# Two edits beside a fused attention and MLP kernel: staging loads issued earlier, and the positive half of an ELU taken by VectorE

## The chip, the cores and the metric

The kernel runs on one core of a Trainium2 chip. Its time is the device time of one execution in microseconds; the time given for a kernel is the median of several executions. Engines are named as in the profile: PE (TensorE), DVE (VectorE), ACT (ScalarE), POOL (GpSimd) and SP (SyncE, which here issues DMAs).

## The reference

Three stages follow each other. An attention with pooled queries (4 batches, 8 heads, 1152 keys, 576 pooled queries, head size 64) gives 2304 tokens of 512 values. A dense MLP multiplies them by a 512x2048 matrix, applies an ELU and multiplies by a 2048x512 matrix. A mixture of 8 experts (512 to 1024 to 512) with top-1 routing follows.

```python
scores = scale * (q_pool @ k.T); attn = softmax(scores); x = attn @ v
h = x @ w_in
g = where(h > 0, h, exp(min(h, 0)) - 1)
y = g @ w_out
# route every row of y to the expert with the largest logit, then
out = gate * (relu(y @ w1[e]) @ w2[e])
```

w_in and w_out arrive as 64-bit floating point words, so the kernel turns them into 32-bit numbers by integer operations on the chip.

## The kernel before

Every product of 32-bit numbers is done in three matmuls over a high and a low part of each operand (H and L). The high part is a rounded copy, usually by ACT, and the low part is the difference, by DVE or POOL.

**Attention** (lines 30 to 330) takes the 16 pairs of heads one after another; a pair is 9 steps, one for each 128 pooled queries, so there are 144 steps, numbered g, and t is the step within its pair (g = 9i + t). The order of the work within a step is written out by hand in SEQ (line 17), and every engine and every DMA queue works in that order. Scores of step g+2 are made (qk, line 164), their maximum is taken by DVE (smax), ACT takes the exponential, PE transposes the probabilities (tp), ACT and DVE split them (evH, evL), and matmuls with v come later from a queue (av_ops). The transposed keys of the next pair, the tile kst, are put together by four DMAs per head from SP: head 0 in step t=4 (D0) and head 1 in step t=7 (D1), both at the operation named inv near the end of a step. PE first reads the new head 0 in step t=7.

Beside the attention, at the operation named dec (line 320), which is third in a step or nearly so, two lists are worked off. The first, pre, decodes weights: two loads of 512 KB into two halves of a staging tile dx (lines 346 and 348), then for each block five DVE operations (lines 351 to 361), an ACT copy and a POOL subtraction or a store; from g=10 on some operations are taken in the steps named in DEC. The second, xops, comes when the first is empty (g=100): for each of the first two chunks of tokens, X.load(n) (line 380) brings attention results from memory into dx, 4 DMAs of 384 KB for chunk 0 and 8 DMAs for chunk 1, and split_ops makes 4 POOL sums (line 417) and 4 splits (lines 419 and 420). The 18 entries are spread evenly up to g=140: X.load(0) falls to g=103 (t=4), its first sum to g=105, X.load(1) to g=123 (t=6).

**The dense MLP** (moe1, line 427) works on 7 chunks of 256 or 384 tokens and on 16 blocks f of 128 hidden values. A unit is a chunk and a block. The first 32 units alternate chunk 0 (384 columns) and chunk 1 (256 columns), because the weight blocks are still being decoded. In unit n PE makes L1 (12 matmuls into a PSUM bank h, of which there are two), then elu runs on it, and PE makes L2 of unit n-3. The elu is min(h,0) by ACT (em), a tanh and an exponential by ACT, one DVE operation that joins them (line 455), and the sum with max(h,0). In chunks 2 to 6 that sum is a second DVE operation that reads h (line 460). In chunks 0 and 1 ACT makes max(h,0) with another pass over h (line 450) into a ring tile, and POOL adds (line 457). The split of the result (gH by ACT, gL by POOL, lines 463 and 464) is queued in fin and issued two units later.

Each elu of the first 32 units also takes two entries of the list dec: words, the five DVE operations of one block of weights and the load of the block after next, and parts, the ACT copy and the POOL subtraction (lines 363 and 365) of the block before. Eight blocks (AHEAD) were decoded beside the attention, so their units have no DVE words; 20 blocks have them.

Of the kernel before, what the change touches and what calls it, by code (L numbers as in the profile page):

```python
# [10 lines left out]
F32=mybir.dt.float32; F32R=mybir.dt.float32r; I32=mybir.dt.int32; U32=mybir.dt.uint32; I64=mybir.dt.int64; BF16=mybir.dt.bfloat16  # L11
AF=mybir.ActivationFunctionType; ALU=mybir.AluOpType; AX=mybir.AxisListType
# [17 lines left out]
def attention(tc, q, k, v, xS, rS, ident, pairs=None, extra=(), start=lambda: None):  # L30
    nc=tc.nc
# [4 lines left out]
    with ctx:  # L36
# [18 lines left out]
        def load(i,what="qkv",eng=None):  # L55
            if i>=len(pairs): return
            b,hp=pairs[i]; h0=2*hp
            d=D_.setdefault(i,dict(ks={},vs={},kst={}))
            for w in what:
                if w=='q':  # L60
                    t=d['qn']=ld.tile([128,KT,2,D],F32,name="qn")
                    (eng or nc.sync).dma_start(out=t,in_=q[b,h0:h0+2].rearrange("h (s r) d -> (h s) (r d)",r=2).rearrange("(t p) x -> p t x",p=128))
                else:
                    t=d[w+'n']=ld.tile([128,2,KT,D],F32,name=w+"n")
                    (eng or nc.sync).dma_start(out=t,in_={'k':k,'v':v}[w][b,h0:h0+2].rearrange("h (p t) d -> p h t d",p=128))
# [98 lines left out]
        def qk(g,n):  # L164
            i,t=divmod(g,9); d=D_[i]
            if g not in st: new(g)
            A=QA[i%2]; Bq=QB[i%2]
            if t==4: L=[(512,0),(640,1)]
            else: L=[(128*t,0)] if t<4 else [(128*t+128,1)]
            ops=[(w[:,c:c+128],h) for c,h in L for w in (A,Bq)]  # L170
            if n==0:
                o=psS.tile([128,2,512],F32,name="Sa"); st[g]['S'][0]=o[:,:,0:384]
                outs=[(o[:,j,0:384],j) for j in range(2)]
            else:
                o=psU.tile([128,384],F32,name="Sb"); st[g]['S'][1]=o
                outs=[(o,2)]
            for o,j in outs:
                for x,(w,h) in enumerate(ops):
                    nc.tensor.matmul(o,w,d['kst'][h][:,j*384:(j+1)*384],start=(x==0),stop=(x==len(ops)-1))  # L179
        def smax(g,n):  # L180
            s=st[g]
            nc.vector.tensor_reduce(out=s['nm'][:,n:n+1],in_=s['S'][n],axis=AX.XY if n==0 else AX.X,op=ALU.max,negate=True)  # L182
        def bias(g):
            nm=st[g]['nm']
            nc.vector.tensor_reduce(out=st[g]['bs'],in_=nm,axis=AX.X,op=ALU.min)  # L185
# [11 lines left out]
        def invT(i,h):  # L197
            a,b=TS[h]; bb,hp=pairs[i]; n=b-a
            T=psT.tile([128,384],F32,name="T",tag="T")
            nc.tensor.transpose(T[0:n,0:128],inv.pop((i,h))[:,1,0:n],ident)  # L200
            o=sm.tile([5,128],F32,name="ro",bufs=1)
            nc.scalar.copy(out=o[0:n],in_=T[0:n,0:128])
            flat=rS[bb][hp:hp+1].rearrange("o h s -> (o h s)")
            nc.sync.dma_start(out=flat[128*a:128*b].rearrange("(t p) -> t p",p=128),in_=o[0:n])
        def invB(i,h):
            bb,hp=pairs[i]
            flat=rS[bb][hp:hp+1].rearrange("o h s -> (o h s)")
            r=rB[i,h]=sm.tile([128,576],F32,name="rB",bufs=2)
            nc.sync.dma_start(out=r,in_=flat[576*h:576*h+576].partition_broadcast(128))
# [48 lines left out]
        N=len(pairs); NG=9*N  # L258
        load(0,'q'); load(0,'k'); load(0,'v',nc.gpsimd)
        def take(l,n=1):  # L260
            for _ in range(n):
                if l: l.pop(0)()
        ops={}
        def do(i,*names):

            if i>=N: return
            if i not in ops: ops[i]=pool_ops(i,i==0)|prep_ops(i)
            for n in names:
                o=ops[i].pop(n,None)
                if o: o()  # L270
# [10 lines left out]
        def takeav(n):  # L281
            while avq and n>0:
                avq[0].pop(0)(); n-=1
                if not avq[0]: avq.pop(0)
        stores=[]; g0=None
        for g in range(NG+4):
            i,t=divmod(g,9)
            if g<NG:
                if t==2 and i>0: load(i+1,'v')
                if t==2: load(i+2,'q')  # L290
                if t==5: load(i+2,'k')
            f2=g+2<NG; f0=g<NG
            if not f0:
                while avq: takeav(99)
            for op in SEQ[t in EARLY]:
                a=op[:-1]; n=op[-1]
                if op=='scl':
                    if g in at: x,y=at.pop(g); x(); stores.append((g,y))
                elif op=='st':
                    while stores and (stores[0][0]<g or not f0): stores.pop(0)[1]()  # L300
                elif op=='inv':
                    if f0 and t in (3,7): invT(i,t//4)
                    if t==5 and f0: invB(i,0)
                    if t==0 and i>0: invB(i-1,1)
                    for di,x in SPQ.get(t,()): f0 and do(i+di,x)
                    if g==0: do(1,'q0')
                elif not f0: pass
                elif a=='q': f2 and qk(g+2,int(n))
                elif a=='m': f2 and smax(g+2,int(n))
                elif a=='e': f2 and exp(g+2,int(n))  # L310
                elif op=='bias': f2 and bias(g+2)
                elif a=='t': tp(g,int(n))
                elif a=='c': evH(g,int(n))
                elif op in ('av','aw'): takeav((AVN[t]+(op=='av'))//2)
                elif a=='l': evL(g,int(n))
                elif op=='sum':
                    if t in (3,7): ssum(i,t//4)
                elif op in ('pool','prep'):
                    for di,n in (POOL if op=='pool' else PREP).get(t,()): do(i+di,n)
                elif op=='dec':  # L320
                    n=DEC.get(t,0) if g>9 else 0
                    while n and extra[0]:
                        d,x=extra[0].pop(0); x(); n-=d
                    if not extra[0]:
                        if g0 is None: g0=g
                        want=min(NX[1],NX[1]*(g-g0)//(140-g0)); take(extra[1],want-(NX[1]-len(extra[1])))
                else: raise Exception(op)
            if f0:
                for c in DONE.get(t,[]): avq.append(av_ops(i,c))
# [97 lines left out]
def moe1(tc, X, yS, R, Wt, dec, rpool, psX, temps, plan, ops, setup, spare):  # L427


    nc=tc.nc  # L430
    ep,gp,psH,psY=temps
    rp=rpool
# [10 lines left out]
    def elu(c,f):  # L443
        h=hs.pop((c,f)); N=CHUNKS[c][1]; h=h[:,:N]
        m=ep.tile([128,384],F32,name="em",bufs=2); t=ep.tile([128,384],F32,name="et",bufs=3); m_,t_=m[:,:N],t[:,:N]
        nc.scalar.activation(out=m_,in_=h,func=AF.Relu,scale=-1.0)  # L446
        if c<2:

            r_=rp.tile([128,512],F32,name="yt",bufs=4)[:,:N]
            nc.scalar.activation(out=r_,in_=h,func=AF.Relu)  # L450
        nc.scalar.activation(out=t_,in_=m_,func=AF.Tanh,scale=-0.5)
        nc.scalar.activation(out=m_,in_=m_,func=AF.Exp,scale=-1.0)  # L452
        if len(fin)>1: fin.pop(0)()
        if c<2: take(dec,1)
        nc.vector.scalar_tensor_tensor(out=t_,in0=m_,scalar=1.0,in1=t_,op0=ALU.add,op1=ALU.mult)  # L455
        if c<2:
            nc.gpsimd.tensor_tensor(out=t_,in0=r_,in1=t_,op=ALU.add)
            take(dec,1)
        else:
            nc.vector.scalar_tensor_tensor(out=t_,in0=h,scalar=0.0,in1=t_,op0=ALU.max,op1=ALU.add)  # L460
        def parts():
            gH=gp.tile([128,384],F32R,name="gH",bufs=2); gL=gp.tile([128,384],F32R,name="gL",bufs=2); gs[c,f]=(gH,gL)
            nc.scalar.copy(out=gH[:,:N],in_=t_)  # L463
            nc.gpsimd.tensor_tensor(out=gL[:,:N],in0=t_,in1=gH[:,:N].bitcast(F32),op=ALU.subtract)  # L464
        fin.append(parts)
# [10 lines left out]
    yt={}  # L476
# [63 lines left out]
    for n in range(len(units)+LAG):  # L540
        if n<len(units):
            c,f=units[n]; nxt=c+1
# [11 lines left out]
        if n>=LAG:  # L554
            c,f=units[n-LAG]
# [23 lines left out]
def take(l,n):  # L579
    for _ in range(n):  # L580
        if l: l.pop(0)()
# [300 lines left out]
def full(tc,q,k,v,w_in,w_out,emb,tau,w1,w2,out,dbg=None):  # L882
    nc=tc.nc
# [6 lines left out]
    with contextlib.ExitStack() as ctx:  # L890
        c=pool(ctx,"c")
# [6 lines left out]
        with tc.manual_schedule():  # L898
# [10 lines left out]
            X=XChunks(nc,xS,[df[:,1536*n:1536*n+1536].rearrange("p (k n) -> p k n",k=4) for n in range(2)])  # L909
# [11 lines left out]
                pre+=[(j<5,x) for j,x in enumerate(ops[n][1])]  # L921
                if n+2<len(ops): pre.append((0,ops[n+2][0]))
            xops=[]
            for n in range(2): xops+=[lambda n=n: X.load(n)]+X.split_ops(n)
            attention(tc,q,k,v,xS,rS,ident,extra=(pre,xops),start=norms)
            wp2=pool(right,"w2",side="right")
            W0.append(wp2.tile([128,2,1024],F32R,name="W2",tag="W2"))
# [1 line left out]
            rp=pool(ctx,"m_r",2)  # L929
# [14 lines left out]
            dec=[]  # L944
# [37 lines left out]
            with contextlib.ExitStack() as tmp:  # L982
# [4 lines left out]
                n=lambda i: i<NSTATIC  # L987
# [56 lines left out]
```

## Time and profile before

| What | us |
|---|---|
| median of three executions | 1339.13 (1337.27 to 1340.05) |
| the profiled execution | 1333.49 |
| its span, first to last instruction | 1331.7 |
| attention | about 0 to 573 |
| dense MLP, chunks 0 and 1 | about 577 to 729 |
| dense MLP, chunks 2 to 6 | about 729 to 1040 |
| experts | about 1040 to 1331 |

Busy time over the span: PE 1225.0, DVE 1080.6, ACT 899.8, POOL 625.0 us. A row of the timeline begins with the start and the duration of an instruction in us; a bracket at its end is the engine's idle time before it and what ended that. In the rows of the windows each engine has its busy time and, in brackets, its instructions; then come the granted TensorE clock as a share of full speed, the mean busy share of the DMA engines and GB/s.

### The profile page before, as it was taken

Reading aid. Unit: us, or ns where it says so; the run is one execution under the profiler, and the core shown is the slowest. Engines: PE = TensorE matmul, PEld = TensorE weight load, DVE = VectorE, ACT = ScalarE, POOL = GpSimd, SP = SyncE. Lnnn points to the kernel's source line nnn. Section 1 sums busy time; section 2 is a strip of 40 time slices with the busy share of each in tenths; the row PEclk is TensorE's granted clock in tenths of the full one; section 3 lists DMA queues with packets and bytes.
Section 4 is the critical chain, followed back from the end, with each engine's and each line's share of the span. In section 5 each row is a group of like instructions: output and inputs, shape, how many; then the busy total and the mean of one; then the engine's idle time right before and its main releaser. Section 6 shows DMA issues by size and latency. Waiting matters only on the chain. (4 is left out here: it accounts for less than half of the span.)

```text
span 1331.7 us, 22409 instructions
## 1 busy us (share of the span) xinstructions
PE 1225.0 (92%) x7341; PEld 1084.4 (81%) x7341; DVE 1080.6 (81%) x1970; ACT 899.8 (68%) x2059; POOL 625.0 (47%) x567
## 2 busy tenths in 40 slices
PE   5889999999999999978779989999999999999996
PEld 4778888888988899866668978888888887788885
DVE  5689999999998788868896797657576889998993
ACT  6778888888888788855546645454556667676672
POOL 3435455444444555347676433333342444455552
PEclk9989999999999899999989999999999999999998
DMA  5446666666666557233432201100102223258710
GB/s 175 115 120 175 159 159 168 168 177 184 167 155 157 152 147 162 70 107 109 118 105 71 86 24 41 28 32 25 39 11 109 82 97 110 95 216 326 264 36 22
DMA packets 121928, 158.53 MB, mean 119 GB/s; under 512 B 12391, under 2 KB 94199, under 8 KB 117456
## 3 DMA queue, kind: packets, MB, share of 16 engines
q1 hardware_dynamic: 117536, 145.13, 38.6%
q0 software_dynamic: 3696, 11.34, 2.4%
q8 instruction: 60, 0.98, 0.3%
q10 hardware_dynamic: 576, 0.59, 0.1%
q14 instruction: 60, 0.49, 0.1%
HBM read 157.58 MB, written 22.37 MB: 135 GB/s over the span
## 5 line engine op out<-in xcount | busy, mean ns | idle before, releaser
L235 DVE TENSOR_TENSOR PL<-T,PH 128x384 fp32r<-128x384 f32 (+1 forms) x480 | 220.7, 509 | 28.5 <-ACT PH L233 28.3
L441 PE MATMUL h<-xH,W 128*128 128x384 f32 (+1 forms) x896 | 222.8, 319 | 15.1 <-DVE et L460 12.5
L233 ACT CAST PH<-T 128x384 fp32r<-128x384 f32 (+1 forms) x480 | 187.3, 457 | 69.6 <-PE T L222 67.7
L464 POOL TENSOR_TENSOR gL<-et,gH 128x384 fp32r<-128x384 f32 (+1 forms) x112 | 111.9, 999 | 202.2 <-ACT gH L463 110.0
L829 DVE TENSOR_TENSOR W<-sg,W 128x2048 fp32r<-128x2048 f32 (+1 forms) x84 | 192.4, 2324 | 16.3 <-ACT W L828 10.7
L441 PEld LDWEIGHTS h<-xH,W 128*128 128x128 f32 x896 | 159.1, 192 | 27.1 <-DVE et L460 20.5
L222 PE MATMUL T<-ident,P 128*128 128x128 f32 x1296 | 168.3, 275 | 0.0
L245 PE MATMUL O<-PH,vs 128*128 128x256 f32 (+1 forms) x576 | 166.4, 311 | 0.6 <-ACT xo L248 0.6
L446 ACT ACTIVATE em<-h 128x384 f32<-128x384 f32 (+1 forms) x112 | 49.9, 446 | 162.0 <-PE h L441 154.3
L245 PE MATMUL O<-PL,vs 128*128 128x256 f32 (+1 forms) x576 | 159.1, 299 | 0.0
L222 PEld LDWEIGHTS T<-ident,P 128*128 128x128 f32 x1296 | 151.6, 141 | 7.4 <-ACT KX L135 1.2
L182 DVE TENSOR_REDUCE nm<-Sa 128x1 f32<-128x768 f32 x144 | 136.5, 948 | 16.2 <-PE Sa L179 12.3
L189 ACT ACTIVATE P<-Sa,bs 128x768 f32<-128x768 f32 x144 | 131.4, 913 | 24.5 <-DVE bs L185 20.2
L441 PE MATMUL h<-xL,W 128*128 128x384 f32 (+1 forms) x448 | 141.8, 316 | 0.0
L455 DVE SCALAR_TENSOR_TENSOR et<-em,et 128x384 f32<-128x384 f32 (+1 forms) x112 | 66.5, 598 | 88.6 <-ACT em L452 86.7
L179 PE MATMUL Sa<-kst,qa 128*128 128x384 f32 x320 | 114.5, 358 | 23.3 <-ACT P L189 23.3
L828 ACT CAST W<-sg 128x2048 fp32r<-128x2048 f32 (+1 forms) x63 | 114.2, 1836 | 11.0 <-DMA sg<-moe_w 11.0
L472 PE MATMUL y<-W,gH 128*128 128x512 f32 x288 | 114.6, 398 | 3.1 <-ACT gH L463 3.1
L475 PE MATMUL y<-W,gL 128*128 128x512 f32 x288 | 87.1, 402 | 28.5 <-POOL gL L464 28.5
L473 PE MATMUL y<-W,gH 128*128 128x512 f32 x288 | 112.9, 392 | 0.0
L250 POOL TENSOR_TENSOR xo<-xo,rB 128x256 f32<-128x256 f32 (+1 forms) x64 | 52.1, 814 | 124.4 <-DMA rB<-rS 87.7
L245 PEld LDWEIGHTS O<-PH,vs 128*128 128x128 f32 x576 | 109.3, 190 | 1.1 <-ACT xo L248 1.1
(298 smaller groups left out, 2975.2 us busy)
## 6 DMA issues: line engine op xcount, KB each, us to landing
sg<-moe_w SPq DMA_DIRECT2D x80, 1024.0 KB
qn<-q SPq DMA_DIRECT2D x16, 576.0 KB
kn<-k SPq DMA_DIRECT2D x16, 576.0 KB
rB<-rS SPq DMA_DIRECT2D x32, 288.0 KB
vn<-v SPq DMA_DIRECT2D x15, 576.0 KB
dx<-moe_w_in SPq DMA_DIRECT2D x16, 512.0 KB
dx<-moe_w_out SPq DMA_DIRECT2D x16, 512.0 KB
qb<-qa SPq DMA_DIRECT2D x64, 96.0 KB
```

What stands on the lines that cost most here:

```text
L179: nc.tensor.matmul(o,w,d['kst'][h][:,j*384:(j+1)*384],start=(x==0),stop=(x==len(ops)-1))
L182: nc.vector.tensor_reduce(out=s['nm'][:,n:n+1],in_=s['S'][n],axis=AX.XY if n==0 else AX.X,op=ALU.max,negate=True)
L189: nc.scalar.activation(out=o,in_=s['S'][n],func=AF.Exp,bias=s['bs'],scale=1.0,accum_out=s['su'][:,n:n+1])
L222: nc.tensor.transpose(T[:,n*128:(n+1)*128],P[:,kt*128:(kt+1)*128],ident)
L233: for H,L,src in parts(g,j): nc.scalar.copy(out=H,in_=src)
L235: for H,L,src in reversed(list(parts(g,j))): nc.vector.tensor_tensor(out=L,in0=src,in1=H.bitcast(F32),op=ALU.subtract)
L245: nc.tensor.matmul(O[0][:,:n],vs[:,kt].rearrange("p a d -> p (a d)"),R[:,kt,:n],start=first,stop=last)
L441: nc.tensor.matmul(h[:,:N],a,b[:,k,:N],start=(n==0),stop=(n==11)); n+=1
L472: nc.tensor.matmul(y,gH[:,sl],wH,start=(f==0),stop=False)
L473: nc.tensor.matmul(y,gH[:,sl],wL,start=False,stop=False)
L828: else: nc.scalar.copy(out=H[:,q],in_=s[:,q])
L829: (nc.gpsimd if (w,j,h) in self.pool_L else nc.vector).tensor_tensor(out=L[:,q],in0=s[:,q],in1=H[:,q].bitcast(F32),op=ALU.subtract)
```

## The change

In attention the first two entries of pre, the loads of the first two weight blocks, are taken in step g=4 instead of g=10. X.load(n) is followed by three empty entries, and xops is taken one entry per step from g=112 on: X.load(0) is then in g=112 (t=4), its first sum in g=116; X.load(1) in g=124 (t=7), its first sum in g=128; the last entry is in g=135. In the MLP the ACT pass and the POOL addition of chunks 0 and 1 go, and DVE's operation of line 460 is used in all chunks.

```diff
                 elif op=='dec':
                     n=DEC.get(t,0) if g>9 else 0
+                    if g==4:
+                        for _ in range(2): extra[0].pop(0)[1]()
                     while n and extra[0]:
                         d,x=extra[0].pop(0); x(); n-=d
                     if not extra[0]:
                         if g0 is None: g0=g
-                        want=min(NX[1],NX[1]*(g-g0)//(140-g0)); take(extra[1],want-(NX[1]-len(extra[1])))
+                        if g>=max(g0,112) and extra[1]: take(extra[1])
...
         nc.scalar.activation(out=m_,in_=h,func=AF.Relu,scale=-1.0)
-        if c<2:
-
-            r_=rp.tile([128,512],F32,name="yt",bufs=4)[:,:N]
-            nc.scalar.activation(out=r_,in_=h,func=AF.Relu)
         nc.scalar.activation(out=t_,in_=m_,func=AF.Tanh,scale=-0.5)
         nc.scalar.activation(out=m_,in_=m_,func=AF.Exp,scale=-1.0)
         if len(fin)>1: fin.pop(0)()
         if c<2: take(dec,1)
         nc.vector.scalar_tensor_tensor(out=t_,in0=m_,scalar=1.0,in1=t_,op0=ALU.add,op1=ALU.mult)
-        if c<2:
-            nc.gpsimd.tensor_tensor(out=t_,in0=r_,in1=t_,op=ALU.add)
-            take(dec,1)
-        else:
-            nc.vector.scalar_tensor_tensor(out=t_,in0=h,scalar=0.0,in1=t_,op0=ALU.max,op1=ALU.add)
+        nc.vector.scalar_tensor_tensor(out=t_,in0=h,scalar=0.0,in1=t_,op0=ALU.max,op1=ALU.add)
+        if c<2: take(dec,1)
...
-            for n in range(2): xops+=[lambda n=n: X.load(n)]+X.split_ops(n)
+            for n in range(2): xops+=[lambda n=n: X.load(n)]+[lambda: None]*3+X.split_ops(n)
```

## Rows read from the trace of the kernel before

**Rows 1.** The page: the span.

```profile
span 1331.7 us, 22409 instructions
```

**Rows 2.** Waits, 60 to 80 us: who waited for whom, total, times, longest.

```profile
DVE dx L351 <- DMA dx<-moe_w_in: 8.5, 1, 8.5
...
PE Sa L179 <- ACT P L189: 8.4, 1, 8.4
```

**Rows 3.** Timeline of SP's DMA issues: start, duration, line, what.

```profile
39.48 0.66 SPq L112 DMA_DIRECT2D kst<-KH  x1
...
54.45 0.43 SPq L204 DMA_DIRECT2D rS<-ro  x1
...
62.75 0.43 SPq L346 DMA_DIRECT2D dx<-moe_w_in  x1
...
81.80 0.28 SPq L204 DMA_DIRECT2D rS<-ro  x1
...
420.97 0.28 SPq L204 DMA_DIRECT2D rS<-ro  x1
...
421.77 3.11 SPq L380 DMA_DIRECT2D dx<-xS  x4
...
443.20 0.43 SPq L204 DMA_DIRECT2D rS<-ro  x1
...
461.11 0.28 SPq L204 DMA_DIRECT2D rS<-ro  x1
...
476.44 0.43 SPq L204 DMA_DIRECT2D rS<-ro  x1
```

**Rows 4.** Windows of 1 us in the attention: engines, clock, DMA share, GB/s.

```profile
69.00:70.00 1.00, 0.00 (x0) 0.00 (x0) 0.96 (x3) 0.00 (x0) 0.00 (x0) 0.50 1.06 385
428.00:429.00 1.00, 1.00 (x11) 1.00 (x10) 0.86 (x2) 0.55 (x3) 0.00 (x0) 1.00 1.11 223
436.00:437.00 1.00, 1.00 (x5) 1.00 (x4) 0.81 (x3) 0.00 (x0) 0.00 (x0) 0.50 1.14 297
```

**Rows 5.** Timeline of PE: first scores of a pair, early and after X.load(0).

```profile
48.55 0.34 PE L179 MATMUL Sb<-kst,qa 128*128 128x384 f32 x1
...
435.03 0.69 PE L179 MATMUL Sb<-kst,qa 128*128 128x384 f32 x1 [4.47 <-DMA kst<-KX]
```

**Rows 6.** Window over the 28 units of the MLP in which words run.

```profile
578.90:712.50 133.60, 103.33 (x530) 87.71 (x529) 113.94 (x133) 71.79 (x167) 94.17 (x86) 0.96 0.36 104
```

**Rows 7.** Waits, 577 to 730 us.

```profile
PE y L475 <- POOL gL L464: 28.5, 17, 2.7
...
DVE dx L351 <- DMA dx<-moe_w_in: 8.1, 4, 4.7
...
DVE dx L351 <- DMA dx<-moe_w_out: 5.6, 4, 2.0
```

**Rows 8.** Timeline of DVE and POOL, one unit's words beside POOL's work.

```profile
609.70 1.49 POOL L365 TENSOR_TENSOR W<-yt,W 128x512 fp32r<-128x512 f32 x1
...
610.06 1.68 DVE L355 SCALAR_TENSOR_TENSOR dx<-dx 128x512 int32<-128x512 int32 x1
...
611.13 1.48 POOL L464 TENSOR_TENSOR gL<-et,gH 128x384 fp32r<-128x384 f32 x1
...
611.77 1.39 DVE L357 SCALAR_TENSOR_TENSOR dx<-dx 128x512 int32<-128x512 int32 x1
...
613.27 0.69 DVE L361 SCALAR_TENSOR_TENSOR yt<-dx 128x512 f32<-128x512 int32 x1
```

**Rows 9.** Lines 457 and 460: duration ns min/median/max, first and last start, forms.

```profile
L457 POOL TENSOR_TENSOR et<-yt,et x32: 733/1042/1340, 585.1 to 728.8; 128x384 f32<-128x384 f32 x16, 128x256 f32<-128x256 f32 x16
...
L460 DVE SCALAR_TENSOR_TENSOR et<-h,et x80: 424/557/559, 731.1 to 1044.9; 128x384 f32<-128x384 f32 x48, 128x256 f32<-128x256 f32 x32
```

**Rows 10.** Timeline of DVE: two units without words between, and chunk 2.

```profile
594.38 0.89 DVE L455 SCALAR_TENSOR_TENSOR et<-em,et 128x384 f32<-128x384 f32 x2
...
738.07 0.56 DVE L455 SCALAR_TENSOR_TENSOR et<-em,et 128x384 f32<-128x384 f32 x1 [2.39 <-ACT em L452]
```

## The prediction

> **What bounds the kernel now.** I read the page first: the span is 1331.7 us [rows 1] and the profiled execution took 1333.49, so 1.8 us lie around it. Its shares of busy time say that PE leads, but they are averages, so I went on by stage: the waits of each stretch, then the timelines where a wait stands out.
>
> Attention is paced by PE, except at two places. At 60 us DVE, whose queue also holds the maxima that the softmax needs, waits 8.5 us for a weight load that SP issued only at 62.75; everything stops with it, and PE stands idle for 8.4 us [rows 2, 3]. The price is best read from marks that recur in each pair, SP's store of the sums (line 204, in steps t=3 and t=7): from t=7 to the next t=3 it took 81.80-54.45 = 27.35 us here, against 461.11-443.20 = 17.91 elsewhere [rows 3], a loss of 9.4 us. That is more than the idle time because PE's granted clock was at 0.50, its lower level of 1.2 GHz, when it began again [rows 4]. The second place is at 430: PE waits 4.47 us for the new keys (kst) [rows 5], whose DMAs were issued behind the four of X.load(0). From t=3 to t=7 it took 443.20-420.97 = 22.23 us, against 476.44-461.11 = 15.33 one pair later [rows 3]: a loss of 6.9 us, again with the clock at 0.50 behind it [rows 4].
>
> In the first two chunks of the MLP PE is busy for only 103 of 133.6 us [rows 6], and waits for POOL's gL, 28.5 us in 17 times [rows 7]. POOL is not the root: DVE is busy for 113.9 and POOL for 94.2 of the same 133.6 us [rows 6], and they hinder each other. A DVE word operation with two inputs from SBUF takes 0.69 us where POOL is idle. The one at 611.77 took 1.39: POOL's subtraction ended at 611.13+1.48 = 612.61, 0.84 us after the start, and the DVE operation ended 0.55 us later; the one at 610.06, begun under another POOL operation, took 1.68 [rows 8]. So each waits until the other has finished. DVE paces the stage, and much of its busy time is waiting for POOL.
>
> **The change, part by part.**
>
> 1. *The first two loads in g=4.* The operation that waited finds its data there long before; the wait, its idle PE and the slow clock after it go: -9.4 us. What is late next there is nothing the rows show; the steps after it ran at the usual pace. But the loads are now queued on SP directly ahead of the first pair's key DMAs: these are issued from 39.48 on, and PE first reads the keys at 48.55 [rows 3, 5], 9.1 us later. X.load(0), some 1.57 MB by its shapes, needed 435.03-421.77 = 13.3 us from its first issue to the keys behind it [rows 3, 5]; at the 223 GB/s of that stretch [rows 4] it took 7.0 of them, which leaves 6.2 for the keys. The two loads are 1.05 MB: 2.7 us at the 385 GB/s at which the same loads moved at 69 us, 4.7 at 223 [rows 4]. The keys then come 8.9 to 10.9 us after the first issue: in time, or 1.8 us late. I take +0.5, and keep 6.9 us (the loss of the other place) as the bad end.
>
> 2. *X.load(0) from g=103 to g=112, X.load(1) from g=123 to g=124.* Both g=103 and g=112 are steps t=4, and in both dec stands ahead of inv, so the four DMAs of X.load(0) are again directly ahead of the key DMAs, which are again needed in t=7. The three empty entries part the load from POOL's first sum, not from the keys. I therefore expect the second stall to move one pair on, to about 470 us, and cost the same: 0 net, with -6.9 as the other end. X.load(1), 8 DMAs, now stands ahead of head 1's keys; those are read only four steps later (some 15 us at 33 to 34 us for 9 steps), against the 13.3 us of the larger load above: 0. It also waits for POOL's last split, one step before; SP's later issues in the list need later work anyway. POOL's stall on the first sum goes, but nothing in the waits of that stretch waited for it: 0.
>
> 3. *ACT's pass and POOL's sum go, DVE reads h* (units 0 to 27, the window of rows 6; the last four units have no words there, and DVE has slack: 0).
>  - Added: 28 operations of line 460, 557 ns for 384 columns and 424 for 256 [rows 9]. Back to back two such operations hide 0.08 us (0.89 for 0.554+0.413, the two forms of line 455 [rows 10]): 14 x (0.48+0.34) = +11.5 us. Their largest time in 80 is 559 ns although POOL works beside many of them [rows 9]: one input comes from PSUM, and they don't wait for POOL.
>  - Relieved: 28 POOL sums of 0.733 us (256 columns, the smallest) or about 1.04 (the median, for 384) [rows 9] = 24.9 us of POOL. DVE was busy 0.853 of the window [rows 6], and of a word operation 0.55 of 0.69 us needs what POOL holds [rows 8]: 24.9 x 0.853 x 0.80 = -17.0 us of waiting inside DVE's operations.
>  - DVE's waits for loads, 8.1+5.6 us in 8 times [rows 7], stand behind units without words. There two more operations now lie between a load's issue and its use, 0.82 us, and of the shortest waits (0.38, 0.73) all goes: -5.7.
>  - A new wait: h is released by DVE and not by ACT, with two banks. L1 of unit n+2 begins after DVE's second operation of unit n; behind it on PE stands L2 of unit n-1. Where words run DVE then has two units of about 4.8 us before it needs the result, and L1 (2.0) and three ACT passes (1.6) take 3.6: 0. Without words cover is thin, and it could cost what rival C says.
>  - ACT loses 14 us and POOL's chain to gL a step, both beside DVE: 0.
>
>  Sum: +11.5-17.0-5.7 = -11.2 us. Bounds: +15.7 (16 x (0.557+0.424), no relief, no cover) and -24.9 (POOL's sums gone whole, nothing added).
>
> [...]
>
> Total: -9.4+0.5+0-11.2 = -20.1 us: 1313.4 against the profiled 1333.49. The median of the runs is 5.6 us above that execution, and the forecast is against the median: 1339.1-20.1 = **1319.0 us**.
>
> **Rivals.**
> - *A, the second stall goes too* (the keys win, or the bandwidth is freer one pair later): -6.9 more, 1312.1. For it: a different pair. Against it: same step, same order on SP.
> - *B, DVE and POOL are one chain:* 113.9+94.2 = 208 us of busy time in 133.6 [rows 6], so a POOL sum removed is won whole and the new operations run beside POOL: -24.9, total -33.8, 1305.3. Against it: PE's own 103 us are then close, and DVE's waits for loads stay.
> - *C, the MLP gains nothing:* holding h makes ACT late and DVE wait as it does in chunk 2 (2.39 us for em [rows 10]). At 8 units without words about 1.4 us each, 11.2 in all: total -8.9, 1330.2. For it: that wait is there in every unit of chunk 2; against it: PE paces that chunk, not this one.
> - *D, slower:* DVE is the pacing engine, and POOL's remaining operations, no longer delayed by sums, meet its words just as often; no relief, and the 15.7 us stand whole, with the load waits: -8.9+15.7 = +6.8, 1345.9. It decides from a relief below some 4 us, since then the attention's gain is spent. Against it: 25 of 94 us of POOL's work are gone.
> - *E, the early loads make the first keys late* as at 430: +6.4 against the forecast, 1325.4. It lies in the forecast's own range.
>
> **How the numbers follow.** Forecast (with E) 0.50, own range 1313 to 1326; A 0.13; B 0.07; C 0.21; D 0.09. The range 1308 to 1332 leaves out most of D, half of B and C's upper part, some 0.2. A difference under 0.2% (2.7 us) can't be told from none: same is 1336.5 to 1341.8. Faster: 0.50+0.13+0.07 and most of C, 0.16 = 0.86; same 0.06 (C's tail, D's lower end); slower 0.08.
>
> **What would show it.** (1) No DVE wait on a load near 60 us, and 17.9 us between the stores at t=7 and t=3 there. (2) A PE wait on kst of about 4.5 us near 460 (470 less the first gain), and none in the pair before. (3) In chunks 0 and 1, no line 457, 28 us less of POOL, line 460 at 557 and 424 ns, DVE's word operations shorter by some 17 us in sum, and PE's waits moved from gL to h (released by line 460). (4) The stage shorter by 8 to 14 us; the later stages only shifted. The forecast is wrong if the keys near 48 us come late, if the stall near 460 is missing, or if DVE's busy time rises in the stage.

## The result, and the profile after

Faster by 15.6 us: 1322.68 us (1321.42 to 1324.91), the kernel before 1338.29 on the same chip; ratio 0.9884, 95% interval 0.9864 to 0.9903. The forecast was 1319.0 (20.1 faster), its range 1308 to 1332. The direction and most of the size were right. The attention gave as much as forecast, the MLP half, and that half not by the path its sum describes (see the part on the prediction).

The profiled execution of before (1333.49) is below all its timed ones, that of after (1324.91) is the slowest of its kind, so their spans differ by only 8.8 us (1322.9 against 1331.7 [rows 1]). The first steps differ too: the first store of the sums is issued at 41.06, before at 39.10, and one more trace below has it at 39.60. I therefore read distances within a trace.

The timeline of SP's DMA issues after (start, duration, line) answers to [rows 3]; line 348 is the first early load, line 382 is X.load.

```profile
41.06 0.28 SPq L204 DMA_DIRECT2D rS<-ro  x1
41.40 0.37 SPq L348 DMA_DIRECT2D dx<-moe_w_in  x1
...
56.87 0.43 SPq L204 DMA_DIRECT2D rS<-ro  x1
...
74.35 0.28 SPq L204 DMA_DIRECT2D rS<-ro  x1
...
415.09 0.28 SPq L204 DMA_DIRECT2D rS<-ro  x1
...
430.41 0.43 SPq L204 DMA_DIRECT2D rS<-ro  x1
...
448.46 0.28 SPq L204 DMA_DIRECT2D rS<-ro  x1
...
449.22 2.61 SPq L382 DMA_DIRECT2D dx<-xS  x4
...
470.42 0.44 SPq L204 DMA_DIRECT2D rS<-ro  x1
```

From t=7 to t=3 after the first pair it is 74.35-56.87 = 17.48 us, against 27.35 before: 9.9 us gone. The pair at 415 takes its normal 15.32 us, and the next one, with X.load(0) in it, 470.42-448.46 = 21.96: the stall has moved one pair on at its old price. PE's timeline after shows both sets of keys behind a load, the early ones 0.20 us late, the others 4.93 (4.47 in [rows 5]).

```profile
50.89 0.44 PE L179 MATMUL Sb<-kst,qa 128*128 128x384 f32 x1 [0.20 <-DMA kst<-KX]
...
462.97 0.52 PE L179 MATMUL Sb<-kst,qa 128*128 128x384 f32 x1 [4.93 <-DMA kst<-KX]
```

For the MLP I take the stretch from the first to the 28th elu's first DVE operation, the one that joins (line 455 before, 453 after). First the window of it before, then after (columns as in [rows 6]).

```profile
583.30:712.10 128.80, 100.66 (x513) 85.24 (x512) 110.18 (x127) 69.22 (x162) 91.87 (x77) 0.96 0.36 104
```

```profile
577.00:701.10 124.10, 101.98 (x505) 88.85 (x505) 114.78 (x154) 61.08 (x136) 67.03 (x54) 0.90 0.37 108
```

It is 4.7 us shorter. POOL has 25 us less, but DVE is busier by 4.6 us, where the forecast had 5.5 less (11.5-17.0). What shrank is DVE's idle time, 18.6 to 9.3 us. The waits of that stretch after:

```profile
PE h L443 <- DVE et L454: 22.0, 11, 4.0
...
DVE et L453 <- ACT em L450: 5.0, 6, 1.5
```

PE's waits have moved from gL [rows 7] to the bank h, as forecast. DVE's waits for loads are 2.1 us (rows below), against 13.7.

DVE's groups by form (count, busy us, mean ns, idle before), first before and then after, show where its time went. Both views hold the words of all 20 blocks, of which the first block's run ahead of the stretch, and the joining operations of 27 units. The first five lines are words (lines 351 to 361 before, 353 to 363 after), then come line 455 or 453 and, after, the added line 454.

```profile
L355 DVE SCALAR_TENSOR_TENSOR dx<-dx 128x512 int32<-128x512 int32 x20 | 25.6, 1282 | 0.7
L353 DVE TENSOR_SCALAR dx<-dx 128x512 int32<-128x512 int32 x20 | 23.1, 1155 | 0.0
L357 DVE SCALAR_TENSOR_TENSOR dx<-dx 128x512 int32<-128x512 int32 x20 | 20.3, 1013 | 0.7
L361 DVE SCALAR_TENSOR_TENSOR yt<-dx 128x512 f32<-128x512 int32 x20 | 17.8, 892 | 1.9
L351 DVE TENSOR_SCALAR dx<-dx 128x512 int32<-128x512 int32 x20 | 11.5, 575 | 19.0 <-DMA dx<-moe_w_in 8.1 <-DMA dx<-moe_w_out 5.6 <-DMA xS<-xo 5.3
L455 DVE SCALAR_TENSOR_TENSOR et<-em,et 128x384 f32<-128x384 f32 x14 | 10.8, 775 | 2.7 <-ACT em L452 2.7
L455 DVE SCALAR_TENSOR_TENSOR et<-em,et 128x256 f32<-128x256 f32 x13 | 5.4, 419 | 0.0
```

```profile
L357 DVE SCALAR_TENSOR_TENSOR dx<-dx 128x512 int32<-128x512 int32 x20 | 18.6, 929 | 0.7
L363 DVE SCALAR_TENSOR_TENSOR yt<-dx 128x512 f32<-128x512 int32 x20 | 18.1, 904 | 0.7
L359 DVE SCALAR_TENSOR_TENSOR dx<-dx 128x512 int32<-128x512 int32 x20 | 17.9, 897 | 0.7
L355 DVE TENSOR_SCALAR dx<-dx 128x512 int32<-128x512 int32 x20 | 16.6, 831 | 0.0
L353 DVE TENSOR_SCALAR dx<-dx 128x512 int32<-128x512 int32 x20 | 14.7, 735 | 7.4 <-DMA xS<-xo 5.3 <-DMA dx<-moe_w_in 1.3 <-DMA dx<-moe_w_out 0.8
L453 DVE SCALAR_TENSOR_TENSOR et<-em,et 128x384 f32<-128x384 f32 x14 | 12.1, 865 | 5.0 <-ACT em L450 5.0
L453 DVE SCALAR_TENSOR_TENSOR et<-em,et 128x256 f32<-128x256 f32 x13 | 9.1, 700 | 0.0
L454 DVE SCALAR_TENSOR_TENSOR et<-h,et 128x384 f32<-128x384 f32 x14 | 7.8, 557 | 0.5
L454 DVE SCALAR_TENSOR_TENSOR et<-h,et 128x256 f32<-128x256 f32 x13 | 5.5, 424 | 0.4
```

All five word operations went from 98.3 to 85.9 us. But the joining operation, which has two inputs from SBUF, went from 16.2 to 21.2 us for 27 of them: its 256-column form from 419 to 700 ns. Part of the waiting for POOL was only handed on. The waits before, 583 to 712 us, show what had kept the joining operation clear of POOL: POOL, which works in the order written, stood idle in front of its sum until the joining operation was done, 14 times and 30.9 us in all.

```profile
POOL et L457 <- DVE et L455: 30.9, 14, 2.9
```

### The profile page after: what moved, and what is told of

The parts are those of the page before. It is cut to its first block, busy times and chain, and to the rows that moved or that the text cites. A ratio compares the mean times of both kernels' runs of the same rounds, so it can differ in the third digit from the quotient of the medians.

```text
span 1322.9 us, 22349 instructions
## 1 busy us (share of the span) xinstructions
PE 1230.1 (93%) x7341; PEld 1092.2 (83%) x7341; DVE 1083.6 (82%) x2002; ACT 889.6 (67%) x2027; POOL 600.5 (45%) x535
## 5 line engine op out<-in xcount | busy, mean ns | idle before, releaser
L443 PE MATMUL h<-xH,W 128*128 128x384 f32 (+1 forms) x896 | 228.5, 326 | 38.1 <-DVE et L454 37.8
L459 POOL TENSOR_TENSOR gL<-et,gH 128x384 fp32r<-128x384 f32 (+1 forms) x112 | 109.1, 974 | 265.8 <-ACT gH L458 134.0
L443 PEld LDWEIGHTS h<-xH,W 128*128 128x128 f32 x896 | 162.3, 196 | 54.1 <-DVE et L454 50.8
L824 DVE TENSOR_TENSOR W<-sg,W 128x2048 fp32r<-128x2048 f32 (+1 forms) x84 | 190.1, 2297 | 17.7 <-ACT W L823 10.2
L453 DVE SCALAR_TENSOR_TENSOR et<-em,et 128x384 f32<-128x384 f32 (+1 forms) x112 | 72.5, 647 | 93.2 <-ACT em L450 93.1
L189 ACT ACTIVATE P<-Sa,bs 128x768 f32<-128x768 f32 x144 | 131.3, 912 | 18.2 <-DVE bs L185 12.2
L467 PE MATMUL y<-W,gH 128*128 128x512 f32 x288 | 116.4, 404 | 1.3 <-ACT gH L458 1.3
L468 PE MATMUL y<-W,gH 128*128 128x512 f32 x288 | 114.5, 398 | 0.0
L179 PE MATMUL Sa<-kst,qb 128*128 128x384 f32 x320 | 109.2, 341 | 0.1
```

Source lines behind the costliest of these rows:

```text
L189: nc.scalar.activation(out=o,in_=s['S'][n],func=AF.Exp,bias=s['bs'],scale=1.0,accum_out=s['su'][:,n:n+1])
L443: nc.tensor.matmul(h[:,:N],a,b[:,k,:N],start=(n==0),stop=(n==11)); n+=1
L467: nc.tensor.matmul(y,gH[:,sl],wH,start=(f==0),stop=False)
L468: nc.tensor.matmul(y,gH[:,sl],wL,start=False,stop=False)
L824: (nc.gpsimd if (w,j,h) in self.pool_L else nc.vector).tensor_tensor(out=L[:,q],in0=s[:,q],in1=H[:,q].bitcast(F32),op=ALU.subtract)
```

## The experiments

Medians; "before" is the kernel before, timed beside the run.

| Run | us | before | ratio (95%) |
|---|---|---|---|
| e1 attention only | 1327.8 | 1338.0 | 0.9925 (0.9909 to 0.9942) |
| e2 MLP only | 1332.5 | 1338.0 | 0.9959 (0.9945 to 0.9973) |
| e3 early loads only | 1328.3 | 1338.0 | 0.9933 (0.9907 to 0.9959) |
| e4 loads clear of the keys | 1314.3 | 1338.0 | 0.9826 (0.9809 to 0.9842) |
| e5 idle POOL sums | 1331.3 | 1337.6 | 0.9959 (0.9946 to 0.9971) |
| e6 no positive half | 1337.9 | 1337.6 | not comparable, see there |
| e7 ACT frees the bank | 1323.0 | 1337.6 | 0.9908 (0.9891 to 0.9926) |
| e8 second bank read | 1333.9 | 1337.6 | 0.9974 (0.9963 to 0.9984) |
| e9 bank freed in last units | 1310.8 | 1337.7 | 0.9796 (0.9782 to 0.9810) |
| e10 also next to units without words | 1316.1 | 1337.7 | 0.9829 (0.9810 to 0.9847) |
| e11 e4 once more | 1315.8 | 1337.7 | 0.9839 (0.9824 to 0.9854) |

**e1 and e2, one part each.** e1 is the changed kernel with the old elu, e2 the kernel before with the new one.

> Only the attention part of the change; the MLP as before. Theory 1 (the forecast's attention step was right at -9, and the MLP gained only 5 of the 11 us): 9 us under before, about 1329.5. Theory 2 (the MLP gained its 11 us, and the attention gave part of its gain back in the slower first steps, 39.10 to 41.06 at the first store of the sums): only 4 to 5 under before, about 1334. In both the wait on the first load is gone and the keys are 4 to 5 us late one pair later.

> Only the MLP part of the change; the attention as before. Theory 1: 5 to 6 us under before, about 1332.5, and the first store of the sums near 39 us. Theory 2: 11 under before, about 1327.

10.2 and 5.5 us faster; together 15.7, the change's 15.6. Theory 1 holds, and within the intervals the parts don't interact. e2's first store of the sums is at 40.85, though its attention is the old one, and e1's at 39.59: the slow first steps come from the execution and not from the change.

**e3, the early loads alone.**

```diff
-                        if g>=max(g0,112) and extra[1]: take(extra[1])
+                        want=min(NX[1],NX[1]*(g-g0)//(140-g0)); take(extra[1],want-(NX[1]-len(extra[1])))
...
-            for n in range(2): xops+=[lambda n=n: X.load(n)]+[lambda: None]*3+X.split_ops(n)
+            for n in range(2): xops+=[lambda n=n: X.load(n)]+X.split_ops(n)
```

(against e1)

> Only the two loads in g=4; the rest as before, X.load(0) in g=103. Theory that the whole attention gain is the first load's (the move of X.load is worth 0): the same as the kernel with the whole attention part, 9 us under before, with the late keys (4.5 us) in the old pair, near 421. Rival (the distance between X.load and POOL's first sum is worth something, since POOL stood 8.6 us there): 2 to 4 us slower than the whole attention part.

1328.3 against e1's 1327.8: the move of X.load is worth nothing within the intervals, although POOL's wait on the first sum (8.5 us here) is gone in e1. The late keys are in the old pair, 4.4 us.

**e4, the loads behind the keys.**

```diff
-                        if g>=max(g0,112) and extra[1]: take(extra[1])
+                        if g>=max(g0,107) and extra[1]: take(extra[1])
...
-            for n in range(2): xops+=[lambda n=n: X.load(n)]+[lambda: None]*3+X.split_ops(n)
+            for n in range(2): xops+=[lambda n=n: X.load(n)]+[lambda: None]*3+X.split_ops(n)+[lambda: None]*(6 if n==0 else 0)
```

> The changed kernel, but X.load(0) is issued in g=107 and X.load(1) in g=125, both steps t=8, behind the key loads and not ahead of them. Theory (the keys are late only because X.load is queued ahead of them): no PE wait on the keys, 6.9 us under the changed kernel, about 1316. Rival (the load's bandwidth collides with whatever comes next, the broadcast of the sums or the value loads): the stall moves to another wait, and the time stays within 2 us of the changed kernel.

1314.3, 8.4 us under the changed kernel by the medians, which were timed apart; by the ratios it is 7.8, and 6.0 in e11, the same kernel once more. SP's timeline of e4 has X.load(0) behind the key DMAs. From t=7 to t=3 across the load it takes 445.72-427.56 = 18.16 us, where [rows 3] have 17.91 without a load, and from t=3 to t=7 461.07-445.72 = 15.35:

```profile
427.56 0.43 SPq L204 DMA_DIRECT2D rS<-ro  x1
...
430.14 0.62 SPq L112 DMA_DIRECT2D kst<-KX  x1
430.80 3.17 SPq L382 DMA_DIRECT2D dx<-xS  x4
...
445.72 0.28 SPq L204 DMA_DIRECT2D rS<-ro  x1
...
461.07 0.43 SPq L204 DMA_DIRECT2D rS<-ro  x1
```

No PE wait on keys is left near the load; two short ones elsewhere in the attention (0.48 and 0.45 us, at 185 and 354 us) have their like in the changed kernel (0.93 and 0.66). X.load(1) moved by one step too, but the changed kernel shows no PE wait on keys behind it. The place in SP's list was the cause, not the distance to POOL.

**e5 to e8, the MLP's terms one by one**, each against the changed kernel.

```diff
# e5, after DVE's second operation (r_ is a ring tile)
+        if c<2:
+            r_=rp.tile([128,512],F32,name="yt",bufs=4)[:,:N]
+            nc.gpsimd.tensor_tensor(out=r_,in0=t_,in1=t_,op=ALU.add)
# e6
-        nc.vector.scalar_tensor_tensor(out=t_,in0=h,scalar=0.0,in1=t_,op0=ALU.max,op1=ALU.add)
+        if c>1: nc.vector.scalar_tensor_tensor(out=t_,in0=h,scalar=0.0,in1=t_,op0=ALU.max,op1=ALU.add)
# e7, behind ACT's first pass
+        if c<2:
+            r_=rp.tile([128,512],F32,name="yt",bufs=4)[:,:N]
+            nc.scalar.activation(out=r_,in_=h,func=AF.Relu)
...
-        nc.vector.scalar_tensor_tensor(out=t_,in0=h,scalar=0.0,in1=t_,op0=ALU.max,op1=ALU.add)
+        if c<2: nc.vector.tensor_tensor(out=t_,in0=r_,in1=t_,op=ALU.add)
+        else: nc.vector.scalar_tensor_tensor(out=t_,in0=h,scalar=0.0,in1=t_,op0=ALU.max,op1=ALU.add)
# e8, ahead of DVE's second operation
+        if c<2:
+            r_=rp.tile([128,512],F32,name="yt",bufs=4)[:,:N]
+            nc.vector.scalar_tensor_tensor(out=r_,in0=h,scalar=0.0,in1=t_,op0=ALU.max,op1=ALU.add)
```

> The changed kernel with an idle POOL sum of the old size after each elu of chunks 0 and 1, into a ring tile that nobody reads: POOL's work is back, its place in the chain is not. The changed kernel stands at 1322.7. Theory R (a POOL sum costs DVE's word operations some 10 us in all, as their rows say, 98.3 to 85.9): 10 us slower, about 1332. Theory L (the forecast's 17 us of relief was right and something else ate it): 17 slower, about 1339. Rival (POOL's work never mattered, only its place in the chain): 0.

> The changed kernel without DVE's second operation in chunks 0 and 1: it leaves the positive half of h out there, and the bank is free after ACT's first pass. Theory R (the second operation stands on DVE's path with its 11.5 us, and holding the bank costs about 3 more): 14 us faster, about 1308. Rival H (the operation is hidden in DVE's waits, and what the stage lost is the held bank): 5 us faster at most, about 1318.

> The changed kernel, but ACT makes max(h,0) in a second pass, as before, and DVE adds it from SBUF: the same count of DVE operations, the bank is freed by ACT, and DVE's second operation now has two inputs from SBUF. Theory R (the held bank costs 3 us, waiting for POOL costs 0.25 us per operation or 7 us): 4 us slower, about 1327. Rival H (the held bank is what ate the missing 6 us): 5 us faster, about 1318.

> The changed kernel with DVE's second operation doubled in chunks 0 and 1 (the first result goes into a ring tile that nobody reads). Theory R (each such operation is on DVE's path at its duration less 0.08): 11.5 to 13 us slower, about 1335. Rival H (DVE has cover for it, since it still waits for ACT in this stage): 2 to 5 us slower, about 1326.

The windows over the stretch of 124.1 us, of e5, e6, e7 and e8 in this order:

```profile
575.20:709.00 133.80, 107.19 (x505) 86.83 (x505) 123.32 (x154) 60.82 (x135) 89.26 (x77) 0.91 0.34 101
```

```profile
574.70:689.40 114.70, 101.45 (x530) 88.54 (x529) 101.30 (x128) 60.62 (x136) 67.98 (x53) 0.96 0.39 117
```

```profile
575.10:701.50 126.40, 103.98 (x532) 88.72 (x530) 122.37 (x155) 68.19 (x164) 69.86 (x54) 0.95 0.35 106
```

```profile
574.20:708.90 134.70, 103.44 (x505) 90.20 (x505) 123.53 (x181) 61.25 (x135) 67.84 (x54) 0.91 0.34 100
```

e5: POOL's 22 us of sums, with no reader, cost 9.7 us of the stretch and 8.6 of the whole: theory R. DVE's busy time carries 8.5 of the 9.7. Its words, 94.9 us in the stretch before and 82.5 in the changed kernel, are back at 94.8; POOL again waits for DVE in front of its sum (34.0 us in 12 times), and the joining operation is shorter again, 17.8 us against 21.2:

```profile
L453 DVE SCALAR_TENSOR_TENSOR et<-em,et 128x384 f32<-128x384 f32 x14 | 11.3, 807 | 0.7 <-ACT em L450 0.7
...
L453 DVE SCALAR_TENSOR_TENSOR et<-em,et 128x256 f32<-128x256 f32 x13 | 6.5, 497 | 0.0
```

So it is POOL's wait in front of its sums that keeps most of its other work off the joining operation. e8: a second read costs 10.6 and 11.2 us: it is on DVE's path at nearly its duration. e6's whole time says nothing, since without the positive half the tokens go to the experts differently (22 blocks of tokens run in its last stage, 21 in the changed kernel); its stretch is 9.4 us shorter, so the second operation with its held bank costs 9.4 there, between rival H's 5 and theory R's 14. e7 settles against rival H: with the bank freed by ACT, DVE's idle time falls from 9.3 to 4.0 us, but its operations take 7.6 more. The whole is the same (0.9908 against 0.9884, the intervals overlap; theory R's 4 us slower is not excluded). From the 28th elu to chunk 2, where words run no longer, it takes 16.5 us against 19.8: the two effects part there, and e9 takes this up.

**e9 to e11, the bank freed only next to units where DVE has no words.**

```diff
# e9, on e4, behind ACT's first pass; in e10 free also where 2*f+c+1 or 2*f+c+2 is in AHEAD
+        free=c<2 and (2*f+c>=26)
+        if free:
+            r_=rp.tile([128,512],F32,name="yt",bufs=4)[:,:N]
+            nc.scalar.activation(out=r_,in_=h,func=AF.Relu)
...
-        nc.vector.scalar_tensor_tensor(out=t_,in0=h,scalar=0.0,in1=t_,op0=ALU.max,op1=ALU.add)
+        if free: nc.vector.tensor_tensor(out=t_,in0=r_,in1=t_,op=ALU.add)
+        else: nc.vector.scalar_tensor_tensor(out=t_,in0=h,scalar=0.0,in1=t_,op0=ALU.max,op1=ALU.add)
```

> The kernel with the loads clear of the keys (1314.3), and in the last six units of chunks 0 and 1, which have no words, ACT makes max(h,0) and DVE adds it from SBUF, so that the bank is free early. Theory (the held bank costs where words give no cover: from the 28th elu to the 33rd 19.8 us with the bank held by DVE and 16.5 with it freed by ACT): 2 to 3 us faster, about 1312. Rival (PE has a backlog there anyway and catches up in chunk 2): within 1 us.

> As the kernel before it, and the bank is also freed by ACT in each unit without words and the one ahead of it. Theory (DVE's waits for ACT, 4 to 5 us in the units with words, come from the held bank next to the units without words, and an addition from SBUF costs 0.2 to 0.3 us more than one from the bank): 1 to 2 us under the kernel before it, about 1310.5. Rival (the additions meet POOL and the words stretch, as they did where all units were freed by ACT): 1 us over it or more.

> The kernel with the loads clear of the keys once more, as the base of the two before it: 0.983 of the kernel before, 1314 to 1315.

Of e9's six units only the last five have no words: in its trace the last block's words still run directly ahead of the first unit's joining operation at 689.40. e9 is 5.0 us under e11 and 3.5 under e4; the interval of its ratio doesn't meet e11's and touches e4's at its edge. It is the fastest of all, 26.9 us under the kernel before. The window from the 28th elu to chunk 2 shows about 3 us, e11 first:

```profile
691.30:709.50 18.20, 18.10 (x100) 16.59 (x101) 7.81 (x16) 10.17 (x24) 4.51 (x5) 1.00 0.25 75
```

```profile
690.50:705.70 15.20, 15.20 (x86) 13.76 (x85) 9.85 (x16) 10.66 (x28) 5.31 (x5) 1.00 0.25 73
```

The theory's base, 19.8 us, came from the profile of the changed kernel, at a granted clock of 0.91; e11 takes 18.2 there at 1.00, and e9 gains 3.0 all the same. PE has 86 matmuls left in the window instead of 100, and 521 instead of 505 in the stretch in front of it, which takes 122.7 us in both: with the bank freed early PE runs ahead. e10 gives the gain back: its stretch takes 127.1 us against 122.7 in e9 and e11, as the rival said.

## Why the prediction was right, and where it was off

The total lies inside the range, 4.5 us short of the forecast. The attention came as it was worked out. In the MLP two of the prediction's own signs came out against it: DVE's busy time rose in the stage (by 4.6 us in the stretch), and the stage became shorter by 4.7 us, not by 8 to 14.

1. *First loads:* right. -9.4 forecast; 9.9 in the trace, 9.7 in e3. The keys behind them came 0.2 us late, inside the 0 to 1.8 that were given (0.67 in e3). The steps from t=3 to t=7 in which they run took 56.87-41.06 = 15.81 us, against 54.45-39.10 = 15.35 before: the +0.5 that I took (0 to 0.9 in e1, e3 and e4).
2. *X.load moved:* right. The stall went one pair on at its price (6.6 against 6.9 us), rival A didn't come, e1 and e3 agree, and e4 shows the cause.
3. *The MLP:* right in direction, half in size (-11.2 forecast, -5.5 in e2), and only partly right in mechanism. The prediction's sum had DVE's operations 5.5 us shorter and its waits 5.7; in the stretch the operations are 4.6 longer and the waits 9.3 shorter.
 - The added operations, +11.5: right (10.6 in e8).
 - The failed term is the relief, -17.0. The words gained 12.4 and chunk 2's sums 1.1 (line 388, 3.9 to 2.8), but the joining operation lost 5.0: about 8.5 net, and 9.7 by e5. That is less than the added operations cost, so on DVE's path the exchange by itself did not pay. I took each us of POOL's sums as gone from DVE's waits. But the sums had also held POOL back until the joining operation was done; without them POOL's other work moved beside operations that had been clear of it. That was rival D's mechanism, at half strength. The share of 0.80 was read from one operation with two inputs; line 353, with one, waited too (421 to 1532 ns before).
 - The load waits, -5.7: they lost 11.6, and the MLP's gain came from here. By the prediction's own rule the term is 6 x 0.82 + 0.38 + 0.73 = 6.0. It counted only the two operations put in front, but the longer joining operations stand there too.
 - The held bank, 0: not quite. DVE's wait for ACT grew from 2.7 to 5.0 us in the stretch. The last units, costed at 0, took 18.4 us before and 18.2 in e11 (19.8 in the profile after, at a clock of 0.91); freeing the bank in another way is worth 3 us there (e9).

One block's load and the word operation that needs it show how the waits for loads shrink, before and then after:

```profile
613.19 0.33 SPq L348 DMA_DIRECT2D dx<-moe_w_out  x1
616.87 1.00 DVE L351 TENSOR_SCALAR dx<-dx 128x512 int32<-128x512 int32 x1 [2.01 <-DMA dx<-moe_w_out]
```

```profile
605.71 0.33 SPq L350 DMA_DIRECT2D dx<-moe_w_out  x1
610.26 0.42 DVE L353 TENSOR_SCALAR dx<-dx 128x512 int32<-128x512 int32 x1
```

Before, DVE was there 1.7 us after the issue (616.87-2.01-613.19) and waited until 3.7. After, it comes after 4.6 us and doesn't wait. Of the 2.9 us between, the two added operations are 1.0 and the longer joining operations 1.7 (1.64+0.90 against 0.89). So part of this gain is the other side of the smaller relief. The prediction's sum had 8.5 us too much relief and 5.9 too little here; it foresaw neither, and that the two partly cancel was luck.

Rival B, POOL and DVE as one chain, is out: e5 puts 22 us of POOL back and pays 9.7.

## What to carry to other kernels

A load that is moved keeps its neighbours in the queue: look at which small transfer stands behind it and when that is read, since the distance to its own reader may be worth nothing (e3) and the order worth 6 to 8 us (e4, e11). When work is taken from an engine that blocks another, price the relief below its full length, because what is left moves up and meets other operations, and look at what the removed work made that engine wait for; putting idle work back (e5) measures it. Between two ways to spend the same operation, choose by unit: reading the bank where the other engine would block, freeing it early where nothing covers the hold.

## What the runs showed that I had not expected

The same joining operation, 419 ns on average before, took 700 after, with nothing of its own changed. Here it is beside POOL, after, DVE's timeline and then POOL's:

```profile
606.74 1.64 DVE L453 SCALAR_TENSOR_TENSOR et<-em,et 128x384 f32<-128x384 f32 x1
608.41 0.56 DVE L454 SCALAR_TENSOR_TENSOR et<-h,et 128x384 f32<-128x384 f32 x1
```

```profile
606.23 1.73 POOL L367 TENSOR_TENSOR W<-dx,W 128x512 fp32r<-128x512 f32 x1
607.91 1.60 POOL L367 TENSOR_TENSOR W<-yt,W 128x512 fp32r<-128x512 f32 x1
```

The operation with two inputs from SBUF took 1.64 us under POOL's, the one with an input from PSUM its usual 0.56. And PE's mean granted clock in the stretch fell from 0.96 to 0.90, although PE had more work in less time; its waits for h are longer (up to 4.0 us) than those for gL were (2.7). PE's timeline, a window of 1 us behind it, and DVE's timeline show one such place after the change:

```profile
609.02 0.44 PE L443 MATMUL h<-xH,W 128*128 128x384 f32 x1 [2.98 <-DVE et L454]
```

```profile
611.00:612.00 1.00, 1.00 (x4) 1.00 (x4) 0.93 (x3) 0.00 (x0) 0.00 (x0) 0.50 0.11 38
```

```profile
614.33 0.56 DVE L453 SCALAR_TENSOR_TENSOR et<-em,et 128x384 f32<-128x384 f32 x1 [1.13 <-ACT em L450]
```

PE waits for the bank, makes most of h at 0.50, its lower level of 1.2 GHz, and DVE then waits for ACT. Three of DVE's six waits for ACT (1.13, 1.47 and 0.49 of the 5.0 us) follow an h that was made mostly at 0.50. How much of them is the clock's wasn't tried apart; e7, whose stretch ran at 0.95, was no faster as a whole.
